# Four sums and a snapshot: who forms the partial sums at the end of the last two blocks

## The chip, the cores and the metric

The kernel runs on one core of one Trainium2 chip. A core has five engines that run their own instruction streams and wait for one another by semaphores: TensorE (PE, matrix products, with PEld for its weight loads), VectorE (DVE), ScalarE (ACT), GpSimd (POOL), and SyncE (SP, which here only issues transfers). The metric is the device time of one execution in microseconds; the profile's span of one execution is a little shorter than that time.

## The reference

Two layers follow one another. The first is a linear attention over 8 batches, 8 heads, 576 rows and 64 columns: `q` is normalised by a softmax along its columns, `k` by one along its rows, and each head's output is `q_s @ (k_s^T @ v)`. The second is a gated feed-forward layer over the 8 x 576 = 4608 rows of 512 values:

```python
x = attn_out.transpose(0, 2, 1, 3).reshape(4608, 512)
g = x @ w_gate                       # 512 x 1536
gelu = 0.5 * g * (1 + erf(g / sqrt(2)))
val = x @ w_val                      # 512 x 1536
out = (gelu * val) @ w_out           # 1536 x 512
```

## The kernel before

The feed-forward layer dominates. Its rows are worked in nine blocks of 512: blocks 0 to 7 are 512 rows of one batch each, and block 8 collects the 64 rows that remain of each batch. The blocks run in the order 0, 1, 2, 3, 4, 5, 6, 8, 7, so that block 7 is the last.

From block 1 on, the output product is a Strassen product in Winograd's form: the hidden values `h` (tile `ht`, twelve column pieces of 128 for 512 rows) and `w_out` are cut into 2 x 2 quarters, and seven products of quarters take the place of eight. They need four sums of quarters of `h`. `NO` is 6: column piece `j` of the left half goes with `j + 6` of the right half.

```python
def sum_h(j0, j1, which, eng="dve"):
    step = 1 if j1 - j0 == 2 else NO // 2          # pair j: pieces j and j + 3
    js, ks = slice(j0, j1, step), slice(NO + j0, NO + j1, step)
    a11, a21 = ht[:, js, 0:256], ht[:, js, 256:512]
    a12, a22 = ht[:, ks, 0:256], ht[:, ks, 256:512]
    s1, s2 = sh[1][:, js], sh[2][:, js]
    for i in which:
        o, a, b, op = {1: (s1, a21, a22, ALU.add), 2: (s2, s1, a11, ALU.subtract),
                       3: (a21, a11, a21, ALU.subtract),
                       4: (s4[:, js], a12, s2, ALU.subtract)}[i]
        (nc.gpsimd if eng == "pool" else nc.vector).tensor_tensor(out=o, in0=a, in1=b, op=op)
```

One call makes each of its sums for two pieces at once, 512 values a partition. There are three such pairs: pair 0 (pieces 0 and 3), pair 1 (1 and 4), pair 2 (2 and 5). Sums 1 and 2 are on VectorE. In blocks 2 to 8, sums 3 and 4 are on GpSimd.

The gate products (`x @ w_gate`, `x @ w_val`) of blocks 8 and 7 are Strassen products too, in twelve column pieces that go in pairs `k` and `k + 3`. The list `SIX` gives their order: `k.i` is step `i` of pair `k`; `s0`, `u0`, `s1`, `u1` are the places where sums of `h` are made. The last steps of a gate pair end in a GELU on ScalarE (`glq`) and a product on VectorE that writes a piece of `ht`:

```python
SIX = ("0.1 6.1 0.2 6.2 0.3 6.3 0.4 1.1 6.4 7.1 s0 1.2 7.2 1.3 u0 7.3 1.4 2.1 7.4 8.1 2.2"
       " 8.2 2.3 s1 8.3 2.4 u1")
# ... (inside pair_step)
def final(ps, fi):
    gl = ffn.tile([P, 256], f32, name="glq", tag="gl")
    nc.scalar.activation(out=gl, in_=ps[:, 1], func=ACTF.Gelu)
    nc.vector.scalar_tensor_tensor(out=ht[:, fi, 0:256], in0=ps[:, 0], scalar=_H_SCALE,
                                   in1=gl, op0=ALU.mult, op1=ALU.mult)
    let_go(ps)
```

The last gate step, `8.4`, is done inside the output stage; it writes the lower rows of piece 11 of `ht`. The upper rows of pieces 8 and 11 come from a VectorE product as well (`ht<-cc` in the profile).

The output stage of a block, cut to what matters (`b == 7` is `last`; there each accumulator is two tiles instead of one):

```python
js = (0, 1, 2, 3, 4, 5) if b < 2 else (0, 3, 1, 4, 2, 5)
get("a")
product(1, ps["a"], True, js=js[:cut])              # cut is 4 in blocks 8 and 7
# ...
if b >= B - 1:
    pair_step(b, get_x(b), NFI - NO // 2 - 1, 4)    # step 8.4
get("b")
product(1, ps["a"], False, js=js[4:])
if b > 1 and not last:
    s1 = snap("a", True)                            # snapshot on ScalarE
ride(b, PR, "e")
sum_h(*last_js(b), (1, 2))                          # pair 2
if b < 2 or last:
    s1 = snap("a")                                  # first tile on VectorE, second on ScalarE
product(2, ps["b"], True, js=js)                    # needs all of ht's lower rows
add("b", s1, 0, 0)
# ...
sum_h(*last_js(b), (4,), "pool" if b > 1 else "dve")
get("c")
product(5, ps["c"], True, js=js)                    # needs sum 1 of all pairs
sum_h(*last_js(b), (3,), "pool" if b > 1 else "dve")
s5 = snap("c", b == B or b == B - 2)
ride(b, NS, 1)
product(6, ps["a"], False, js=js)                   # needs sum 2, and the snapshot s1 done
s2 = snap("a", b == B or b == B - 2)
ride(b, NS, 2)
product(3, ps["c"], False, js=js[:cut])             # needs sum 4
# ... then product 7 (needs sum 3) and product 4
```

A `product` is twelve matrix products of 256 columns. `ride(b, NS, i)` is a place where work for later blocks may be put; in block 1 two sums of quarters of the gate weights lie at place 2:

```python
at(1, NS, 2, L(sum_wgv, "g", 3), L(sum_wgv, "v", 3))
# ...
for b in range(2, B + 1):
    for j in range(NO // 2 - 1):
        at(b, PR, f"s{j}", L(sum_h, j, NO, (1,)), L(sum_h, j, NO, (3,), "pool"))
        at(b, PR, f"u{j}", L(sum_h, j, NO, (2,)), L(sum_h, j, NO, (4,), "pool"))
```

Of the kernel before, what the change touches and what calls it, by code (L numbers as in the profile page):

```python
# [18 lines left out]
def kernel(  # L19
# [12 lines left out]
    B, H, S, D = q.shape  # L32
# [16 lines left out]
    NO = NFI // 2  # L49
# [30 lines left out]
    def big(shape, dt, name, hold=False, seed=False):  # L80
        tag = ring.pop(next(i for i, x in enumerate(ring) if x in full) if seed else 0)
        t = ps_big.tile(shape, dt, name=name, tag=tag)
        words = 1
        for n in shape[1:]:
            words *= n
        (full.add if words == 512 and shape[0] == 128 and dt == f32 else full.discard)(tag)
        if hold:
            held[id(t)] = (t, tag)
        else:
            ring.append(tag)  # L90
        return t

    def let_go(t):
        ring.append(held.pop(id(t))[1])
# [471 lines left out]
    def sum_h(j0, j1, which, eng="dve"):  # L566
        step = 1 if j1 - j0 == 2 else NO // 2
# [9 lines that stand above are left out]
# [18 lines left out]
    def product_gv(i, ps, xt, k, first):  # L595
# [3 lines left out]
        for t, w, nm in ((0, wv_sb, "v"), (1, wg_sb, "g")):  # L599
# [13 lines left out]
    FOUR = ("a 7g l 7v n 0.1 6.1 0.2 6.2 0.3 6.3 m 10g 0.4 6.4 1.1 t 10v 1.2 s0 8g u0 1.3 8v 1.4 2.1"  # L613
            " 11g s1 2.2 11v 2.3")
    SIX = ("0.1 6.1 0.2 6.2 0.3 6.3 0.4 1.1 6.4 7.1 s0 1.2 7.2 1.3 u0 7.3 1.4 2.1 7.4 8.1 2.2"
           " 8.2 2.3 s1 8.3 2.4 u1")
    steps = {b: (SIX if b >= B - 1 else THREE if b == 2 else FOUR).split() for b in range(2, B + 1)}
    live = {}

# [88 lines left out]
    def product(i, ps, first, ts=(0, 1), js=range(NO)):  # L708
        for j in js:
            for t in ts:  # L710
                c0, c1 = slice(t * P, (t + 1) * P), slice(256 + t * P, 256 + (t + 1) * P)
                a = {1: ht[:, j, c0], 2: ht[:, NO + j, c0], 3: s4[:, j, c0], 4: ht[:, NO + j, c1],
                     5: sh[1][:, j, c0], 6: sh[2][:, j, c0], 7: ht[:, j, c1]}[i]
                w = {1: wo_sb[:, j, 0:256], 2: wo_sb[:, NO + j, 0:256],
                     3: wo_sb[:, NO + j, 256:512]}.get(i)
                if w is None:
                    w = tw[{4: 4, 5: 1, 6: 2, 7: 3}[i]][:, j]
                nc.tensor.matmul(ps[t], a, w, start=(first and j == js[0] and (  # L718
                    t == ts[0] or ps[t].tensor is not ps[ts[0]].tensor)),
                                 stop=(j == js[-1]), skip_group_check=True)  # L720

    def get_x(b):
        return get_xt(b) if b < B else xtr

    def last_js(b):
        return (NO - 2 if b < 2 else NO // 2 - 1, NO)

    def out_strassen(b, last):
        yo = [yop.tile([P, 2, C], f32, name="yo", tag="yo") for _ in range(2)]
        c = (slice(0, 256), slice(256, 512))  # L730
        ps, tiles_ = {}, {}

        def get(nm):
            if last:
                tiles_[nm] = [big([P, 256], f32, "ps" + nm, True) for _ in range(2)]
                ps[nm] = [x for x in tiles_[nm]]
            else:
                tiles_[nm] = [big([P, 2, 256], f32, "ps" + nm, True)]
                ps[nm] = [tiles_[nm][0][:, t] for t in range(2)]

        def parts(nm):
            return [(0, ps[nm][0]), (1, ps[nm][1])] if last else [(slice(0, 2), tiles_[nm][0])]

        def snap(nm, act=False):
            sn = ffn.tile([P, 2, 256], f32, name="sn", tag="gl")
            for n, (t, src) in enumerate(parts(nm)):
                if n or act:
                    nc.scalar.activation(out=sn[:, t], in_=src, func=ACTF.Copy, scale=1.0 / _H_SCALE)
                else:
                    nc.vector.tensor_scalar(out=sn[:, t], in0=src, scalar1=1.0 / _H_SCALE,  # L750
                                            scalar2=None, op0=ALU.mult)
            return sn

        def add(nm, sn, half, col):
            for t, src in parts(nm):
                nc.vector.scalar_tensor_tensor(  # L756
                    out=yo[half][:, t, c[col]], in0=src, scalar=1.0 / _H_SCALE,
                    in1=sn[:, t], op0=ALU.mult, op1=ALU.add)

        js = (0, 1, 2, 3, 4, 5) if b < 2 else (0, 3, 1, 4, 2, 5)  # L760
        get("a")
        four = 2 < b < B - 1
        cut = 3 if four else 4
        product(1, ps["a"], True, js=js[:cut])
        if four:
            pair_step(b, get_x(b), NO // 2 - 1, 4)
            product(1, ps["a"], False, js=js[cut:4])
        ride(b, NS, 0)
        if four:
            ride(b, PR, "u1")  # L770
        if b >= B - 1:
            pair_step(b, get_x(b), NFI - NO // 2 - 1, 4)
        get("b")
        product(1, ps["a"], False, js=js[4:])
        if b > 1 and not last:
            s1 = snap("a", True)
        ride(b, PR, "e")
        sum_h(*last_js(b), (1, 2))
        if b < 2 or last:
            s1 = snap("a")  # L780
        product(2, ps["b"], True, js=js)
        add("b", s1, 0, 0)
        for x in tiles_["b"]:
            let_go(x)
        sum_h(*last_js(b), (4,), "pool" if b > 1 else "dve")
        get("c")
        product(5, ps["c"], True, js=js)
# [3 lines that stand above are left out]
        product(6, ps["a"], False, js=js)  # L791
        s2 = snap("a", b == B or b == B - 2)
        ride(b, NS, 2)
        cut = NO - 1 if 1 < b < B - 2 else NO
        product(3, ps["c"], False, js=js[:cut])
        if cut < NO:
            product(7, ps["a"], False, js=js)
            add("a", s5, 1, 1)
            product(3, ps["c"], False, js=js[cut:])
        add("c", s2, 0, 1)  # L800
        for x in tiles_["c"]:
            let_go(x)
        store_rows(b, 0, yo[0])
        if last:
            finish_last(b, ps["a"], yo[1], s5)
            return
        if cut == NO:
            product(7, ps["a"], False, js=js)
            add("a", s5, 1, 1)
        ride(b, NS, 4)  # L810
        if b == B:
            go_on(B - 1, get_x(B - 1), 1)
        product(4, ps["a"], False, js=js)
        nc.scalar.activation(out=yo[1][:, :, c[0]], in_=tiles_["a"][0], func=ACTF.Copy,
                             scale=1.0 / _H_SCALE)
        let_go(tiles_["a"][0])
        store_rows(b, 1, yo[1])
# [16 lines left out]
    def store_rows(b, half, yo):  # L834
        if b < B:
            store(nc.sync, yo.rearrange("p n c -> p (n c)"), b, 2 * half, 2 * half + 2)
            return
        for t in range(2):
            for j in range(2):
                o = 2 * (2 * half + t) + j  # L840
                nc.sync.dma_start(
                    out=out[o * S:(o + 1) * S, :].rearrange("(m n) c -> m n c", n=NT)[:, 0, :],
                    in_=yo[j * 64:(j + 1) * 64, t, :])
# [71 lines left out]
    FI, NS, PR = range(3)  # L915
    plan = {}

    def at(b, kind, i, *fns):
        plan.setdefault((b, kind, i), []).extend(fns)

    L = lambda f, *a: (lambda: f(*a))
# [35 lines left out]
    for i, x in enumerate(("g1", "v1", "g2", "v2", "g4", "v4")):  # L957
        at(0, FI, 5 + i, L(sum_wgv, x[0], int(x[1])))
    at(0, FI, NFI - 2, L(sum_w, 1))
    at(1, NS, 2, L(sum_wgv, "g", 3), L(sum_wgv, "v", 3))  # L960
    for b in range(2, B):
        n = b + 1
        if n < B:
# [19 lines left out]
    at(B, NS, 2, L(lambda: sum_x(get_x(B - 1), xs_b[1])))  # L983
    for b in range(2, B + 1):
        for j in range(NO // 2 - 1):
            at(b, PR, f"s{j}", L(sum_h, j, NO, (1,)), L(sum_h, j, NO, (3,), "pool"))
            at(b, PR, f"u{j}", L(sum_h, j, NO, (2,)), L(sum_h, j, NO, (4,), "pool"))
    for i, xs_ in (("w", ("g1", "v1", "g2", "v2")), ("x", ("g4", "v4", "g3", "v3"))):
        for x in xs_:
            at(2, PR, i, L(sum_wgv, x[0], int(x[1]), NO, 1, "pool"))  # L990
# [5 lines left out]
    def ride(b, kind, i):  # L996
        for fn in plan.get((b, kind, i), []):
            fn()
# [63 lines left out]
```

The softmax here doesn't subtract the row's maximum and nothing guards it: scores larger than these inputs give would overflow.

## Time and profile before

| | before |
|---|---|
| time, median of 3 (lowest to highest) | 296.51 us (296.48 to 296.78) |
| span of the profiled execution | 294.7 us |
| TensorE busy | 283.5 us (96%) |
| TensorE weight loads busy | 202.8 us (69%) |
| VectorE busy | 226.0 us (77%) |
| GpSimd busy | 205.9 us (70%) |
| ScalarE busy | 194.4 us (66%) |

A line of the timeline has the start in us from the span's beginning, the duration, the engine, the line of the kernel, the operation with `out<-in` by tile name, shapes, how many instructions were merged, and in brackets the idle time before and what ended it. Names to know: `psa`, `psb`, `psc` are the accumulators of the output stage; `sh` holds sums 1 and 2, `s` sum 4, and sum 3 overwrites its quarter of `ht`; `sn` is a snapshot of an accumulator, `yo` a result. `L576` is the line of the sums of `h`, `L587` that of the weight sums, `L718` that of the output products. Consecutive instructions of VectorE overlap a little: one starts about 0.08 us before the end that the profile gives for the one ahead. [...]what counts for TensorE is the distance from start to start.

### The profile page before, as it was taken

The numbers are of one execution on the slowest core, as the hardware profiler recorded it, in microseconds if no ns is written. First come the engines' busy times: TensorE is split into PE (matmuls) and PEld (weight loads), VectorE is DVE, ScalarE is ACT, GpSimd is POOL, SyncE is SP. The second block draws the span as 40 slices with busy tenths as digits, with TensorE's granted clock in tenths as the row PEclk, the third lists the DMA queues.
The fourth block names the chain that finished last, engine by engine and source line by source line (L and its number), as shares of the span: only waits on it lengthen the run. The fifth ranks groups of instructions, "written<-read, shape, count | busy, mean of one in ns | idle before, by whom it ended". The sixth has DMA issues, their size and how long they took to land. (4 is left out here: it accounts for less than half of the span.)

```text
span 294.7 us, 6354 instructions
## 1 busy us (share of the span) xinstructions
PE 283.5 (96%) x2449; PEld 202.8 (69%) x2449; DVE 226.0 (77%) x409; ACT 194.4 (66%) x321; POOL 205.9 (70%) x191
## 2 busy tenths in 40 slices
PE   3999999999999999999999999999999999899984
PEld 1544445446767687779777877687768888788863
DVE  2855888878878769768977896787678789849992
ACT  4663367776776589768976898589863576447730
POOL 1558647870499699868887788779886555774480
PEclk9999999999999999999999999999999999999999
DMA  6999999998069605970499039803050200032003
GB/s 225 373 382 389 400 391 392 337 323 231 3 224 383 108 3 174 382 157 3 153 373 206 2 136 350 232 1 122 24 100 2 120 24 1 2 91 55 0 2 142
DMA packets 54622, 51.72 MB, mean 176 GB/s; under 512 B 18496, under 2 KB 50496, under 8 KB 54592
## 3 DMA queue, kind: packets, MB, share of 16 engines
q1 hardware_dynamic: 52864, 49.49, 52.9%
q10 hardware_dynamic: 1728, 1.84, 1.9%
q8 instruction: 19, 0.31, 0.4%
q14 instruction: 11, 0.09, 0.1%
HBM read 37.75 MB, written 9.44 MB: 160 GB/s over the span
## 5 line engine op out<-in xcount | busy, mean ns | idle before, releaser
L467 PE MATMUL psg<-xt,wg_sb 128*128 128x512 f16 x184 | 49.3, 379 | 0.0
L467 PE MATMUL psv<-xt,wv_sb 128*128 128x512 f16 x184 | 49.2, 379 | 0.0
L718 PEld LDWEIGHTS <-ht 128*128 128x128 f16 x384 | 36.4, 98 | 10.1 <-issue 2.7
L250 POOL TENSOR_TENSOR eq<-eq,rrq 128x640 f16<-128x640 f16 (+1 forms) x27 | 34.7, 1302 | 11.7 <-DVE rrq L242 7.8
L576 POOL TENSOR_TENSOR ht<-ht 128x512 f16<-128x512 f16 x21 | 26.7, 1270 | 6.1 <-DVE sh L576 6.1
L606 PEld LDWEIGHTS <-wv_sb 128*128 128x128 f16 x248 | 24.1, 98 | 9.4 <-issue 1.0
L653 POOL TENSOR_TENSOR ht<-eq 128x512 f16<-128x512 f32 x14 | 17.8, 1273 | 18.0 <-ACT eq L651 18.0
L467 PEld LDWEIGHTS <-wv_sb 128*128 128x128 f16 x184 | 17.9, 98 | 18.0 <-issue 0.5
L576 POOL TENSOR_TENSOR s<-ht,sh 128x512 f16<-128x512 f16 x21 | 24.7, 1176 | 6.9 <-DVE sh L576 6.9
L467 PEld LDWEIGHTS <-wg_sb 128*128 128x128 f16 x184 | 17.9, 98 | 16.5
L634 DVE SCALAR_TENSOR_TENSOR ht<-pga,glq 128x256 f16<-128x256 f32 x31 | 13.0, 421 | 20.6 <-ACT glq L633 20.5
L188 POOL CAST v<-vt 128x640 f16<-128x640 f32 x26 | 19.1, 776 | 12.8 <-PE pskv L343 11.3
L606 PEld LDWEIGHTS <-wg_sb 128*128 128x128 f16 x248 | 24.2, 98 | 2.8
L653 POOL TENSOR_TENSOR ht<-cc 128x512 f16<-128x512 f32 x15 | 19.1, 1274 | 8.6 <-ACT cc L651 8.5
L472 ACT ACTIVATE gl<-psg 128x512 f32<-128x512 f32 x24 | 13.8, 597 | 16.9 <-PE psg L467 15.8
L633 ACT ACTIVATE glq<-pgb 128x256 f32<-128x256 f32 x31 | 11.7, 378 | 18.7 <-PE pgb L606 10.9
L718 PE MATMUL psa<-tw,ht 128*128 128x256 f16 x192 | 23.4, 272 | 0.2 <-DVE yo L756 0.2
L212 ACT ACTIVATE ek<-kt 128x1280 f16<-128x1280 f32 (+1 forms) x11 | 19.1, 1748 | 5.7 <-DMA kt<-in_k_dram 4.2
L473 DVE SCALAR_TENSOR_TENSOR ht<-psv,gl 128x512 f16<-128x512 f32 x24 | 16.0, 686 | 8.6 <-PE psv L467 6.8
L663 ACT COPY pgb<-pga 128x512 f32<-128x512 f32 x31 | 18.0, 580 | 6.9 <-PE pga L606 6.6
L643 ACT ACTIVATE snq<-pga 128x512 f32<-128x512 f32 x31 | 18.5, 599 | 4.0 <-PE pga L606 3.7
L718 PEld LDWEIGHTS <-sh 128*128 128x128 f16 x192 | 18.6, 98 | 2.8 <-DVE sh L576 0.4
(172 smaller groups left out, 732.0 us busy)
## 6 DMA issues: line engine op xcount, KB each, us to landing
out_dram<-yo SPq DMA_DIRECT2D x15, 512.0 KB, 3.4
kt<-in_k_dram SPq DMA_DIRECT2D x7, 640.0 KB, 8.6
vt<-in_v_dram SPq DMA_DIRECT2D x7, 640.0 KB, 5.0
qt<-in_q_dram SPq DMA_DIRECT2D x7, 640.0 KB, 7.6
qt<-in_q_dram SPq DMA_DIRECT2D x8, 512.0 KB, 7.8
wost<-in_moe_w_out_dram SPq DMA_DIRECT2D x6, 512.0 KB, 7.9
kt<-in_k_dram SPq DMA_DIRECT2D x6, 512.0 KB, 9.7
vt<-in_v_dram SPq DMA_DIRECT2D x6, 512.0 KB, 5.7
```

The source lines that it names most:

```text
L188: nc.gpsimd.tensor_copy(out=dst, in_=src)
L212: nc.scalar.activation(out=dst[:, n0:NC, h0 * D:h1 * D].rearrange(o, d=D, **({"t": 2} if b >= QUAD else {})), in_=heads(tiles[(nm, b)], b, ...
L250: (nc.gpsimd if eng == "pool" else nc.vector).tensor_tensor(out=e, in0=e, in1=rrq.unsqueeze(-1).to_broadcast((P, n, 2, D)), op=ALU.mult)
L467: nc.tensor.matmul(ps, w[:, ci, fi * P:(fi + 1) * P], xt[:, ci, :], start=(ci == 0), stop=(ci == HP - 1))
L472: nc.scalar.activation(out=gl, in_=psg, func=ACTF.Gelu)
L473: nc.vector.scalar_tensor_tensor(out=ht[:, fi, :], in0=psv, scalar=_H_SCALE, in1=gl, op0=ALU.mult, op1=ALU.mult)
L576: (nc.gpsimd if eng == "pool" else nc.vector).tensor_tensor(out=o, in0=a, in1=b, op=op)
L606: nc.tensor.matmul(ps[:, t], a, x, start=(first and t == 0 and c == 0), stop=(c == 1), skip_group_check=True)
L643: nc.scalar.activation(out=sn, in_=ps, func=ACTF.Copy, scale=_H_SCALE)
L653: (nc.vector if k == NFI - NO // 2 - 1 else nc.gpsimd).tensor_tensor(out=ht[:, k:k + NO // 2 + 1:NO // 2, 256:512], in0=cc[:, :, 0], in1=c ...
L663: nc.scalar.copy(out=pb, in_=pa)
L718: nc.tensor.matmul(ps[t], a, w, start=(first and j == js[0] and (t == ts[0] or ps[t].tensor is not ps[ts[0]].tensor)), stop=(j == js[-1]), ...
```

## The change

Three things are moved; nothing is computed that was not computed before, and nothing is left out.

1. In blocks 8 and 7 the sums 3 and 4 of pair 1 go from GpSimd to VectorE. Together with sum 2 they now stand in the output stage behind the first sum of pair 2, so that the last gate piece of `ht` comes ahead of them.
2. The first snapshot of block 7 is made on ScalarE alone, as it is in blocks 2 to 6 and 8, and before the sums in the program.
3. In block 1 the sum of the gate weights `g` moves from place 2 to place 1 of the output stage, one snapshot earlier.

The first is meant to take VectorE and GpSimd out of each other's way in the last output stages and to let TensorE have its last piece of `ht` earlier; the second relieves VectorE of an instruction there; the third uses a pause of VectorE.

```diff
@@ the order of the gate steps
-           " 8.2 2.3 s1 8.3 2.4 u1")
+           " 8.2 2.3 s1 8.3 2.4")
@@ the output stage
-        if b > 1 and not last:
+        if b > 1:
             s1 = snap("a", True)
         ride(b, PR, "e")
-        sum_h(*last_js(b), (1, 2))
-        if b < 2 or last:
+        sum_h(*last_js(b), (1,))
+        if b >= B - 1:
+            ride(b, PR, "u1")
+        sum_h(*last_js(b), (2,))
+        if b < 2:
             s1 = snap("a")
@@ the plan
-    at(1, NS, 2, L(sum_wgv, "g", 3), L(sum_wgv, "v", 3))
+    at(1, NS, 1, L(sum_wgv, "g", 3))
+    at(1, NS, 2, L(sum_wgv, "v", 3))
@@
-            at(b, PR, f"s{j}", L(sum_h, j, NO, (1,)), L(sum_h, j, NO, (3,), "pool"))
-            at(b, PR, f"u{j}", L(sum_h, j, NO, (2,)), L(sum_h, j, NO, (4,), "pool"))
+            at(b, PR, f"s{j}", L(sum_h, j, NO, (1,)))
+            if j and b >= B - 1:
+                at(b, PR, f"u{j}", L(sum_h, j, NO, (2, 3, 4)))
+            else:
+                at(b, PR, f"s{j}", L(sum_h, j, NO, (3,), "pool"))
+                at(b, PR, f"u{j}", L(sum_h, j, NO, (2,)), L(sum_h, j, NO, (4,), "pool"))
```

## The prediction

> **What bounds the kernel now.** I read four views, from the whole to the instruction. The page comes first. TensorE has work in 283.5 of 294.7 us (96%) at the full clock, and only the first slice and a few late ones are below 9 tenths, so time can be won only where TensorE stands still. The waits of TensorE between 60 us and the end are the second view. They are three lines:
>
> ```profile
> PE psb L718 <- DVE ht L634: 1.8, 2, 0.9
> PE psa L718 <- DVE yo L756: 0.2, 1, 0.2
> PE psa L718 <- DVE sn L750: 0.2, 1, 0.2
> ```
>
> Columns are total us, number of waits, longest. The reader is to see that two waits of 0.9 us carry nearly all of it, and that each names a VectorE write of `ht`. The third view, the timeline, puts one of them at 254.77 us (block 8) and one at 283.56 us (block 7, the last to run). Around the latter it reads (start, duration, engine, line, operation, count, idle before):
>
> ```profile
> 279.97 1.28 POOL L653 TENSOR_TENSOR ht<-eq 128x512 f16<-128x512 f32 x1 [2.55 <-ACT eq L651]
> ...
> 281.19 0.69 DVE L653 TENSOR_TENSOR ht<-cc 128x512 f16<-128x512 f32 x1
> 281.21 1.68 POOL L576 TENSOR_TENSOR ht<-ht 128x512 f16<-128x512 f16 x1
> 281.22 0.38 ACT L633 ACTIVATE glq<-pga 128x256 f32<-128x256 f32 x1
> 281.40 1.26 PE L718 MATMUL psb<-wo_sb,ht 128*128 128x256 f16 x10
> ...
> 281.80 1.37 DVE L576 TENSOR_TENSOR sh<-sh,ht 128x512 f16<-128x512 f16 x1
> 283.09 0.41 DVE L634 SCALAR_TENSOR_TENSOR ht<-pga,glq 128x256 f16<-128x256 f32 x1
> 283.25 1.15 POOL L576 TENSOR_TENSOR s<-ht,sh 128x512 f16<-128x512 f16 x1 [0.36 <-DVE sh L576]
> 283.43 1.25 DVE L576 TENSOR_TENSOR sh<-ht 128x512 f16<-128x512 f16 x1
> ...
> 283.56 0.39 PE L718 MATMUL psb<-wo_sb,ht 128*128 128x256 f16 x2 [0.91 <-DVE ht L634]
> ...
> 283.79 1.56 PE L718 MATMUL psc<-tw,sh 128*128 128x256 f16 x12
> 284.71 0.42 DVE L576 TENSOR_TENSOR sh<-sh,ht 128x512 f16<-128x512 f16 x1
> ...
> 285.06 0.42 DVE L750 TENSOR_SCALAR sn<-psa 128x256 f32<-128x256 f32 x1
> ...
> 285.53 1.47 PE L718 MATMUL psa<-tw,sh 128*128 128x256 f16 x12 [0.18 <-DVE sn L750]
> ```
>
> Read it from the late end. The last two of the 12 `psb` products need the last piece of `ht`, which VectorE writes at 283.09. Its input `glq` was there at 281.60 (281.22 + 0.38). VectorE was held by the sum in front of it: `sh<-sh,ht` at 281.80, for 1.37 us, where its median is 0.42. GpSimd's `ht<-ht` runs over the same time, until 282.89, and VectorE's sum ends 0.28 us after it. At 283.25 and 283.43 the same pair collides again: GpSimd's `s` ends at 284.40, VectorE's `sh` (1.25 us) at 284.68. Only then can the next `sh` and the first snapshot (285.06) go, and the `psa` products wait for that snapshot until 285.53.
>
> What that costs TensorE, with one product per 0.109 us (12 `psa` products of block 8 at 256.40 are followed by `psc` at 257.71: 1.31 / 12). In block 7 ten `psb` products from 281.40 are issued by 282.49, and the next start at 283.56: 1.07 lost. Twelve `psc` from 283.79 would end at 285.10, and `psa` starts at 285.53: 0.43 lost. Afterwards 1.30 us lie between groups, nothing lost. In block 8 the ten from 252.61 should be followed at 253.70 and are at 254.77: 1.07 lost; then 0.09, as `psc` at 255.00 is followed by `psa` at 256.40. So 1.50 us in block 7 and 1.16 us in block 8.
>
> The remaining 0.2 us is at the end of block 1:
>
> ```profile
> 76.71 3.36 POOL L188 CAST v<-vt 128x640 f16<-128x640 f32 x4 [11.34 <-PE pskv L343]
> ...
> 77.65 0.84 DVE L587 TENSOR_TENSOR wg_sb<-wg_sb 128x768 f16<-128x768 f16 x1
> ...
> 78.42 1.06 DVE L587 TENSOR_TENSOR wv_sb<-wv_sb 128x768 f16<-128x768 f16 x1
> ...
> 80.01 0.67 DVE L756 SCALAR_TENSOR_TENSOR yo<-psa,sn 128x512 f32<-128x512 f32 x1
> ...
> 80.74 1.47 PE L718 MATMUL psa<-tw,ht 128*128 128x256 f16 x12 [0.21 <-DVE yo L756]
> ```
>
> Two weight sums of VectorE lie between the snapshot and the two results `yo`; the second `yo` begins at 80.01 although its products ended at 79.79, and the next `psa` group waits for it.
>
> **What the Trainium skill says.** "SBUF — State Buffer", section "Who interferes with whom": a VectorE instruction with two SBUF inputs and a GpSimd instruction that reads SBUF take an exclusive lock in turn, and the later one fully blocks. The trace agrees: 1.37 and 1.25 us against 0.42, each ending just behind GpSimd's instruction, and GpSimd's 1.68 against a median 1.16 where it started behind VectorE's `ht<-cc` (281.19 to 281.88). "VectorE: DVE Perf Modes", section "The TRN2 errata": 58 + elements / mode cycles at 0.96 GHz. For 512 two-byte elements at twice the rate that gives 314 cycles, an estimated 327 ns from one sum to the next; the trace has 0.33 us where two unblocked sums follow (74.33 and 74.66). "GPSIMD Engine Reference", section 4.1, calls GpSimd about half as fast for two inputs; here it is worse, 1.15 against 0.42 us.
>
> **The change, part by part.**
>
> 1. Sums 3 and 4 of pair 1 in blocks 8 and 7 leave GpSimd: 2 x 2 instructions of 1.15 us when unblocked, more when not. VectorE gets them at 0.33 us from start to start, two more per block, 0.66 us. Sum 2 of pair 1, which was already VectorE's, moves behind the gate product and the first sum of pair 2. The instruction order confirms the new sequence: `ht<-cc`, `ht<-pga`, sum 1 of pair 2, sums 2, 3, 4 of pair 1, sum 2 of pair 2, `yo<-psb`.
>
> Worked on the times of block 7. `ht<-cc` starts at 281.19 as before, as it waits for ScalarE. The next can start 0.61 later (281.80, as now), and is now `ht<-pga`: 281.80 to 282.21, seen by TensorE 0.06 later (as 283.50 was seen at 283.56), 282.27. TensorE wants it at 282.49, and its weight load about 0.1 earlier, at 282.38. It fits, with some 0.1 us to spare, so the whole 1.07 goes. Block 8: 253.01 to 253.42, wanted at about 253.59: the same.
>
> Then the five sums start at 282.13, 282.46, 282.79, 283.12, 283.45, and the last ends at 283.88. No GpSimd sum is left to collide with: its `ht<-eq` ends at 281.25, its next sum waits for 283.88. TensorE, undisturbed, starts `psc` at 282.71, needs the late half of `sh` 1 at 283.58 (ready 282.54), starts `psa` at 284.02, needs the late half of `sh` 2 at 284.89 (ready 283.88), starts the next `psc` at 285.33 and wants GpSimd's last `s` at 286.20. GpSimd can do that from about 283.95 to 285.10 and its last `ht` to 286.25, wanted at 286.86. So 0.43 in block 7 and 0.09 in block 8 go too. VectorE then still has two `yo<-psb` (0.76) and half a snapshot of `psc` (0.42) after 283.88, done by 284.90, wanted at 285.33.
>
> 2. The first snapshot of block 7 on ScalarE: one VectorE instruction of 0.42 less, one ScalarE instruction of 0.38 more, ready at about 282.40 where ScalarE is idle for 3.34 us. It removes what `psa` waited for at 285.53. Its gain is in the 0.43 already counted. Block 8 had its snapshot there already.
>
> 3. The weight sum of block 1 moves into the gap before the snapshot (75.72 to 76.34, 0.62 us idle). GpSimd is idle there until 76.71, so I take 0.55 us for it, from the same shape at 27.4 us (548 ns), and it just fits. The remaining weight sum then runs from 77.65 and ends near 78.6, `yo<-psc` can follow its products (78.5), and `yo<-psa` starts with its own at 79.83 instead of 80.01. That is 0.18 us at the `psa` group; 0.03 of the 0.21 stays.
>
> Sum: 1.50 + 1.16 + 0.18 = 2.84 us, and 296.51 - 2.84 = 293.67.
>
> **The rivals.** First: a wait is moved and not removed. The new run of sums pushes the release of `psb` and the snapshot of `psc` later, or the 0.1 us to spare at the gate product is not there. For it speaks that VectorE goes without a pause for 4 us; against it the margins above, 0.4 us or more everywhere but at the gate product. It would leave 0.1 to 0.4 us per block: 294.0 to 294.5. Second: VectorE is so slowed by five sums in a row that it becomes the bound of the output stage. If each took 0.46 us from start to start (as 71.89 to 72.35, where one needs its predecessor's result), the last would end at 284.4, the snapshot of `psc` at 285.4, 0.1 late: 293.9. The order separates sums that depend on one another by another instruction, except the first move from `ht<-pga` to sum 1. Third: what is won in block 1 or 8 is lost later, since GpSimd's `vt` sums feed block 7 and loads feed blocks 2 to 4. The waits list shows no TensorE wait on either, and the `vt` sums start as much earlier as TensorE does (GpSimd loses 2.3 us of work before them). If the block 1 gain is lost, 293.85. Fourth: a new collision of the moved weight sum; it would take 0.84 or more, and the snapshot behind it would start 0.2 us late with no one waiting.
>
> **Range and chances.** All known disturbances take from the gain, so the range leans upward: 293.7 us, between 293.3 and 294.6. To reach 2% it would need 5.9 us, and TensorE has no more than 2.9 us of such waits after 60 us; to lose 2% a new wait of 5.9 us would have to arise. I give 1% to each.
>
> **What would show it.** In the profile after, the line of `psb` waiting for `ht` is gone or under 0.2 us in sum; the pair 1 sums of blocks 8 and 7 take about 0.42 us each on VectorE, none over 0.6; `psb`, `psc`, `psa` and `psc` follow one another at 1.31 us in both blocks; GpSimd has four instructions less. The span falls from 294.7 to about 291.9. A remaining gap before the last two `psb` products would prove the first rival; sums over 0.45 us and a wait for `sn` the second; an end of block 1 that is earlier by under 0.1 us would show step 3 wrong.

## The result and the profile after

The changed kernel takes 293.73 us (293.70 to 293.77, four runs) against 296.60 us (296.48 to 296.78, four runs) of the kernel before. The ratio is 0.9903, with a 95% interval of 0.9886 to 0.9920. The prediction was 293.7 us. The span went from 294.7 to 292.0 us.

The page of the changed kernel (span; busy time of TensorE; its busy tenths in 40 slices):

```profile
span 292.0 us, 6352 instructions
...
PE 282.8 (97%) x2449; PEld 203.1 (70%) x2449; DVE 221.8 (76%) x412; ACT 194.9 (67%) x322; POOL 200.5 (69%) x187
...
PE   3999999999999999999999999999999999999994
```

TensorE has a 9 in every slice but the first and the last. Its waits over the whole span (total us, times, longest) are now two, both before 60 us:

```profile
engine line waited for: us in total, times, longest us
PE pswarm L459 <- ACT warm L864: 4.9, 1, 4.9
PE pst L368 <- POOL eq L250: 0.3, 1, 0.3
```

The two waits of `psb` for `ht`, and the waits of `psa` for `sn` and `yo`, are gone. The timeline of block 7's output stage shows the new order (start, duration, engine, line, operation, count, idle before):

```profile
279.93 0.69 DVE L653 TENSOR_TENSOR ht<-cc 128x512 f16<-128x512 f32 x1
279.96 0.38 ACT L633 ACTIVATE glq<-pga 128x256 f32<-128x256 f32 x1
280.14 1.47 PE L718 MATMUL psb<-wo_sb,ht 128*128 128x256 f16 x12
280.29 0.66 ACT L748 ACTIVATE sn<-psa 128x256 f32<-128x256 f32 x2
280.54 0.42 DVE L634 SCALAR_TENSOR_TENSOR ht<-pga,glq 128x256 f16<-128x256 f32 x1
280.87 0.41 DVE L576 TENSOR_TENSOR sh<-ht 128x512 f16<-128x512 f16 x1
281.20 0.42 DVE L576 TENSOR_TENSOR sh<-sh,ht 128x512 f16<-128x512 f16 x1
...
281.45 1.47 PE L718 MATMUL psc<-tw,sh 128*128 128x256 f16 x12
281.54 0.42 DVE L576 TENSOR_TENSOR ht<-ht 128x512 f16<-128x512 f16 x1
281.87 0.42 DVE L576 TENSOR_TENSOR s<-ht,sh 128x512 f16<-128x512 f16 x1
282.21 0.42 DVE L576 TENSOR_TENSOR sh<-sh,ht 128x512 f16<-128x512 f16 x1
...
282.70 1.16 POOL L576 TENSOR_TENSOR s<-ht,sh 128x512 f16<-128x512 f16 x1 [2.73 <-DVE sh L576]
282.76 1.47 PE L718 MATMUL psa<-tw,sh 128*128 128x256 f16 x12
...
284.07 1.47 PE L718 MATMUL psc<-wo_sb,s 128*128 128x256 f16 x12
```

`ht<-pga` starts at 280.54, directly behind `ht<-cc`, and not behind a sum; the twelve `psb` products are one group. The five sums stand 0.33 us apart and take 0.41 or 0.42 us each. GpSimd's next instruction is at 282.70, when they are all done. The groups of TensorE start at 280.14, 281.45, 282.76 and 284.07: 1.31 us apart each time, which is twelve products without a pause.

**Where the time came from.** The start of every group of TensorE products can be compared with the same group of the kernel before. The difference stays constant over long stretches and jumps only where something was won or lost. The prologue before 60 us moves from one execution to the next, by up to 0.3 us in all traces but one, so only the jumps count:

| place (time in the kernel before) | changed kernel against before | jump |
|---|---|---|
| 60.54, block 1 | -0.05 us | (prologue) |
| 80.74, `psa` at the end of block 1 | -0.22 us | 0.17 us won |
| 108.82, `psa` at the end of block 2 | -0.11 us | 0.11 us lost |
| 171.17, block 4 | -0.09 us | 0.02 us lost |
| 255.00 and 256.40, `psc`, `psa` of block 8 | -1.18, then -1.27 us | 1.18 us won |
| 283.79 and 285.53, `psc`, `psa` of block 7 | -2.34, then -2.77 us | 1.50 us won |

The sum of the jumps is 0.17 - 0.11 - 0.02 + 1.18 + 1.50 = 2.72 us. Blocks 8 and 7 gave what was forecast. Block 1 gave it too, but two thirds of that was lost again within 28 us, at a place where the kernel before seemed to have no wait. The theory for blocks 8 and 7 was the collision of the two engines plus the order of VectorE's instructions; what was open was how much each of the two is worth. For the loss in block 2, the two traces name GpSimd. Here is the kernel before at that place (PEld is the weight load of TensorE):

```profile
100.86 1.27 POOL L653 TENSOR_TENSOR ht<-cc 128x512 f16<-128x512 f32 x1 [1.78 <-ACT cc L651]
100.87 1.54 DVE L576 TENSOR_TENSOR sh<-sh,ht 128x512 f16<-128x512 f16 x1
...
102.09 1.34 POOL L576 TENSOR_TENSOR ht<-ht 128x512 f16<-128x512 f16 x1
...
107.37 1.16 POOL L576 TENSOR_TENSOR s<-ht,sh 128x512 f16<-128x512 f16 x1
...
107.67 1.31 PE L718 MATMUL psc<-wo_sb,s 128*128 128x256 f16 x10
...
108.58 0.11 PEld L718 LDWEIGHTS <-s 128*128 128x128 f16 x2 [0.15 <-POOL s L576]
...
108.82 1.50 PE L718 MATMUL psa<-tw,ht 128*128 128x256 f16 x12
```

and here the changed kernel:

```profile
100.64 1.56 POOL L653 TENSOR_TENSOR ht<-cc 128x512 f16<-128x512 f32 x1 [1.73 <-ACT cc L651]
100.65 0.43 DVE L576 TENSOR_TENSOR sh<-sh,ht 128x512 f16<-128x512 f16 x1
...
102.17 1.15 POOL L576 TENSOR_TENSOR ht<-ht 128x512 f16<-128x512 f16 x1
...
107.26 1.16 POOL L576 TENSOR_TENSOR s<-ht,sh 128x512 f16<-128x512 f16 x1
...
107.45 1.42 PE L718 MATMUL psc<-wo_sb,s 128*128 128x256 f16 x10
...
108.47 0.11 PEld L718 LDWEIGHTS <-s 128*128 128x128 f16 x2 [0.27 <-POOL s L576]
...
108.71 1.50 PE L718 MATMUL psa<-tw,ht 128*128 128x256 f16 x12
```

Ten `psc` products should take 1.09 us to issue; before, `psa` follows after 1.15, now after 1.26. The last two of them need the `s` that GpSimd starts at 107.37 before and 107.26 now. TensorE came 0.22 us earlier, GpSimd only 0.11. The reason is at the top of each fence: two instructions start within 0.01 us of one another, GpSimd's `ht<-cc` and VectorE's `sh`. Before, VectorE was blocked (1.54 us); now GpSimd was, and took 1.56 us in place of 1.27. So its next sum starts 0.08 us later than before (102.17 against 102.09), although `ht<-cc` had started 0.22 earlier; that sum then wins 0.19 us back (1.15 us in place of 1.34). From there to 109 us GpSimd works without a pause in both kernels, so the rest of the delay reaches `s`.

This loss does not hang on the moved weight sum alone. The kernel before with only the snapshot of block 7 moved (its run is below) has nothing changed before block 7. In its trace the same two instructions start at the same times as in the kernel before, yet GpSimd is the one that is blocked:

```profile
100.86 1.56 POOL L653 TENSOR_TENSOR ht<-cc 128x512 f16<-128x512 f32 x1 [1.78 <-ACT cc L651]
100.87 0.42 DVE L576 TENSOR_TENSOR sh<-sh,ht 128x512 f16<-128x512 f16 x1
...
108.69 0.11 PEld L718 LDWEIGHTS <-s 128*128 128x128 f16 x2 [0.26 <-POOL s L576]
...
108.93 1.50 PE L718 MATMUL psa<-tw,ht 128*128 128x256 f16 x12
```

Its `psa` starts at 108.93 in place of 108.82: the same 0.11 us are lost, with nothing won in block 1. Of the ten traces with block 2 as it was, `psa` follows `psc` after 1.24 to 1.26 us in the five where GpSimd is blocked, and after 1.14 to 1.15 us in the five where VectorE is. The four of these ten that have the weight sum moved are all among the first five; of the six that have it at its old place, one is (the snapshot alone). Whether the moved sum tips the balance, or chance, is not shown.

### The profile page after: what moved, and what is told of

It reads as the page before. It is cut to its first block, busy times and chain, and to the rows that moved or that the text cites. A ratio compares the mean times of both kernels' runs of the same rounds, so it can differ in the third digit from the quotient of the medians.

```text
span 292.0 us, 6352 instructions
## 1 busy us (share of the span) xinstructions
PE 282.8 (97%) x2449; PEld 203.1 (70%) x2449; DVE 221.8 (76%) x412; ACT 194.9 (67%) x322; POOL 200.5 (69%) x187
## 4 chain that ended last, share of the span: by engine, by line
PE 94%; DVE 2%; DMA 2%; ACT 0%; issue 0%; ACTq 0%
PE pga L606 19%; PE psa L718 15%; PE psg L467 14%; PE psv L467 14%; PE pgc L606 9%; PE psc L718 7%; PE pgb L606 5%; PE psb L718 4%; PE psy L535 4%; DMA qt<-in_q_dram 2%; PE pskv L343 2%; PE psx L430 1%; DVE rq L240 1%; PE psx L409 1%; DVE eq L250 0%; PE pskv L284 0%
## 5 line engine op out<-in xcount | busy, mean ns | idle before, releaser
L576 POOL TENSOR_TENSOR s<-ht,sh 128x512 f16<-128x512 f16 x19 | 22.4, 1178 | 9.8 <-DVE sh L576 9.8
L576 POOL TENSOR_TENSOR ht<-ht 128x512 f16<-128x512 f16 x19 | 23.1, 1215 | 6.1 <-DVE sh L576 6.1
L240 DVE TENSOR_REDUCE rq<-eq 128x20 f32<-128x1280 f16 (+1 forms) x12 | 17.2, 1432 | 4.6 <-ACT eq L212 4.6
```

What stands on the lines that cost most here:

```text
L240: nc.vector.reduce_sum(rq, e, axis=mybir.AxisListType.X)
```

## The experiments

All are compared with the kernel before, on the same chip as they ran. "Jump" means the shift of TensorE's groups, as above.

**The sums alone.** The changed kernel with the snapshot and the weight sum as before:

```diff
-        if b > 1:
+        if b > 1 and not last:
             s1 = snap("a", True)
...
-        if b < 2:
+        if b < 2 or last:
             s1 = snap("a")
...
-    at(1, NS, 1, L(sum_wgv, "g", 3))
-    at(1, NS, 2, L(sum_wgv, "v", 3))
+    at(1, NS, 2, L(sum_wgv, "g", 3), L(sum_wgv, "v", 3))
```

> The sums of pair 1 alone (part 1), snapshot and weight sum as before. My theory: the wait before the last two psb products goes in both blocks (1.07 us each) and block 8 has its full 1.16 us. In block 7 the first half of the snapshot is still VectorE's, behind five sums: it would end at 284.22 on the clock of the kernel before, where psa is wanted at 284.02, so about 0.26 us stay. Gain 1.16 + 1.50 - 0.26 = 2.40 us, about 294.2 us. The rival, that the snapshot did not matter once the sums are free, expects 2.66 us, about 293.9 us.

Measured: 294.10 us (294.04 to 294.17), before 296.54; ratio 0.9915 (0.9900 to 0.9929). The jumps are 1.16 us in block 8, 1.07 at `psc` and 0.17 at `psa` in block 7: 1.24 us. The first half of the snapshot runs at 282.59 to 283.01 and `psa` starts at 283.06, where 1.31 us behind `psc` (281.49) would be 282.80: 0.26 us, as expected. Behind the five sums the place of the snapshot matters.

**The snapshot alone.** The kernel before with `if b > 1:` and `if b < 2:` at the two places.

> The first snapshot of block 7 on ScalarE alone (part 2) on the kernel before. My theory: the 0.43 us before the psa group in block 7 shrinks to the 0.09 us that block 8 shows with its ScalarE snapshot, and nothing else moves: a gain of 0.34 us, 296.2 us. The rival that this wait is the sums' and not the snapshot's expects no change.

Measured: 296.20 us (295.99 to 296.45), before 296.49; ratio 0.9990 (0.9982 to 0.9998). The only jump at the end is at `psa` of block 7, from +0.15 to -0.20: 0.35 us. (0.11 of the +0.15 is the loss in block 2 shown above.) So the two parts overlap: alone the snapshot is worth 0.35 us, behind the sums 0.26.

**The order alone.** The changed kernel with sums 3 and 4 of pair 1 on GpSimd:

```diff
-            at(b, PR, f"s{j}", L(sum_h, j, NO, (1,)))
-            if j and b >= B - 1:
-                at(b, PR, f"u{j}", L(sum_h, j, NO, (2, 3, 4)))
-            else: ...
+            at(b, PR, f"s{j}", L(sum_h, j, NO, (1,)), L(sum_h, j, NO, (3,), "pool"))
+            at(b, PR, f"u{j}", L(sum_h, j, NO, (2,)), L(sum_h, j, NO, (4,), "pool"))
```

> The changed kernel with sums 3 and 4 of pair 1 in blocks 8 and 7 back on GpSimd: the new order alone. My theory: the gate product, which reads one operand from SBUF only, needs no lock, so ahead of the sums it is early and both waits of 1.07 us go. GpSimd then has 2 x 1.15 us more before its last two sums, and the psc and psa groups behind them wait some 0.3 to 0.7 us per block: about 294.4 to 294.9 us. The rival that the lock is all, and that the order without the engine does little, expects the two waits of 0.9 us back and about 296.4 us. The rival that order is all expects 293.75 us.

Measured: 294.00 us (293.93 to 294.05), before 296.54; ratio 0.9911 (0.9894 to 0.9927). That is faster than I expected, and much nearer to the rival that order is all. The timeline of its block 7:

```profile
279.90 0.69 DVE L653 TENSOR_TENSOR ht<-cc 128x512 f16<-128x512 f32 x1
279.91 1.69 POOL L576 TENSOR_TENSOR ht<-ht 128x512 f16<-128x512 f16 x1
...
280.51 0.42 DVE L634 SCALAR_TENSOR_TENSOR ht<-pga,glq 128x256 f16<-128x256 f32 x1
280.84 1.04 DVE L576 TENSOR_TENSOR sh<-ht 128x512 f16<-128x512 f16 x1
...
284.64 1.15 POOL L576 TENSOR_TENSOR ht<-ht 128x512 f16<-128x512 f16 x1
...
285.35 3.10 PE L718 MATMUL psa<-tw,ht 128*128 128x256 f16 x24
```

The collision is there in full: GpSimd's `ht<-ht` takes 1.69 us and ends at 281.60, and VectorE's first `sh` takes 1.04 us, ending 0.28 us later. But the gate product between them, `ht<-pga` at 280.51, takes 0.42 us while GpSimd runs. It has one operand in PSUM and one in SBUF. The Trainium skill says as much ("SBUF — State Buffer", "Who interferes with whom"): a VectorE instruction with at most one SBUF input, outside its two-port modes, does not contend. The blocked sums have slack and the gate product has none, so putting it first is enough: the jumps are 1.17 us in block 8 and 1.51 us in block 7, as in the changed kernel. What GpSimd still costs comes at the very end: its last `ht<-ht` starts at 284.64 and ends at 285.79, and the 24 `psa` products that read it take 3.10 us where the changed kernel has 2.81: 0.29 us. In block 7 the third of these products needs it already, in block 8 only the ninth, and there nothing is lost. My 0.3 to 0.7 us per block was right for one block, at its lower end.

**The engine alone.** The kernel before, with

```diff
+            if j and b >= B - 1:
+                at(b, PR, f"s{j}", L(sum_h, j, NO, (1, 3)))
+                at(b, PR, f"u{j}", L(sum_h, j, NO, (2, 4)))
+                continue
             at(b, PR, f"s{j}", L(sum_h, j, NO, (1,)), L(sum_h, j, NO, (3,), "pool"))
```

> The kernel before with only the engine changed: sums 3 and 4 of pair 1 in blocks 8 and 7 on VectorE at their old places. My theory: no sum is blocked any more (all near 0.42 us), but three sums stand ahead of the gate product, and the extra one at the earlier place delays the upper rows too; the last psb products are still about 0.9 us late. Gain about 0.28 us in block 8 and 0.62 us in block 7, about 295.7 us. The rival that the lock is all expects the waits for ht gone and about 294 us.

Measured: 295.91 us (295.77 to 295.98), before 296.54; ratio 0.9977 (0.9967 to 0.9987). The jumps are 0.12 us in block 8 and 0.46 in block 7, a little less than expected. Its waits of TensorE after 60 us:

```profile
PE psb L718 <- DVE ht L634: 0.9, 2, 0.4
PE pga L606 <- DVE cc L647: 0.5, 2, 0.3
PE psa L718 <- DVE yo L756: 0.2, 1, 0.2
```

No sum is blocked, yet `psb` still waits for `ht`, and there is a new wait: sum 3 at its old place pushes `cc` back, and the last gate products (`pga`) wait for it. The part of the wait that was a collision became plain work in the wrong place.

**The collision alone.** The kernel before without sums 3 and 4 of pair 1 in blocks 8 and 7. They are left out, so those blocks multiply old values of `s` and unchanged quarters of `ht`; the number of products is the same.

```diff
+            if j and b >= B - 1:
+                at(b, PR, f"s{j}", L(sum_h, j, NO, (1,)))
+                at(b, PR, f"u{j}", L(sum_h, j, NO, (2,)))
+                continue
             at(b, PR, f"s{j}", L(sum_h, j, NO, (1,)), L(sum_h, j, NO, (3,), "pool"))
```

> The kernel before without sums 3 and 4 of pair 1 in blocks 8 and 7 (left out, so those two blocks multiply stale values): nothing else is moved. My theory: sum 2 takes 0.42 us in place of 1.37, the gate product ends at 282.54 on the clock of the kernel before, and the last two psb products are about 0.1 us late instead of 1.07. Gain about 1.04 us in block 8 and 1.38 us in block 7, about 294.2 us. The rival that it is the place of sum 2 in the order that costs, and not the collision, expects the wait to stay near 0.9 us and no gain to speak of.

Measured: 293.93 us (293.87 to 294.23), before 296.54; ratio 0.9911 (0.9896 to 0.9926). Jumps 1.04 us in block 8 and 1.38 in block 7, both as expected. The time is lower than the 294.2 expected: 296.54 less the two jumps is 294.12, and in the trace TensorE was 0.14 us early before block 8. Block 7:

```profile
280.01 0.69 DVE L653 TENSOR_TENSOR ht<-cc 128x512 f16<-128x512 f32 x1
...
280.23 1.60 PE L718 MATMUL psb<-wo_sb,ht 128*128 128x256 f16 x12
...
280.62 0.42 DVE L576 TENSOR_TENSOR sh<-sh,ht 128x512 f16<-128x512 f16 x1
280.96 0.41 DVE L634 SCALAR_TENSOR_TENSOR ht<-pga,glq 128x256 f16<-128x256 f32 x1
...
281.66 1.47 PE L718 MATMUL psc<-tw,sh 128*128 128x256 f16 x12
```

Sum 2 still stands ahead of the gate product, but takes 0.42 us. The twelve `psb` products are one group of 1.60 us where 1.47 would be undisturbed: the 0.1 us that sum 2 costs by its place. So of the 1.07 us per block, the collision made up all but that. The first half of the snapshot is still VectorE's here, at 282.08 with two sums fewer ahead of it, and `psa` at 282.97 does not wait for it.

**The weight sum alone.** The kernel before with `at(1, NS, 1, L(sum_wgv, "g", 3))` taken out of place 2.

> The weight sum of block 1 alone (part 3) on the kernel before. My theory from the two traces: the psa group at the end of block 1 is 0.17 us earlier, but at the end of block 2 the psc group waits for GpSimd's sum of pair 2, whose chain is only 0.06 us earlier net, so that about 0.06 to 0.1 us of 0.18 reach the end: 296.4 to 296.55 us. The rival that the whole 0.18 us is kept expects 296.35 us and a constant shift of 0.17 us after block 1.

Measured: 296.48 us against 296.49, ratio 0.9997 (0.9989 to 1.0006): no difference can be measured. In its trace, whose prologue came 2.5 us late, the shift goes from +2.50 to +2.33 at the end of block 1 (0.17 won), to +2.42 at the end of block 2 (0.09 lost), and to +2.46 at the end. GpSimd is blocked in block 2 here too (1.56 us), and little is kept.

**The loss in block 2.** Two weight sums of GpSimd (0.67 us each) stand ahead of its last two sums of `h` in block 2, and are needed only in block 3. In this version of the changed kernel they stand behind them:

```diff
-    for i, xs_ in (("w", ("g1", "v1", "g2", "v2")), ("x", ("g4", "v4", "g3", "v3"))):
+    for i, xs_ in (("w", ("g1", "v1", "g2", "v2")), ("x", ("g4", "v4"))):
         for x in xs_:
             at(2, PR, i, L(sum_wgv, x[0], int(x[1]), NO, 1, "pool"))
+    at(2, NS, 1, L(sum_wgv, "g", 3, NO, 1, "pool"), L(sum_wgv, "v", 3, NO, 1, "pool"))
```

> The changed kernel with two of GpSimd's weight sums at the end of block 2 (g3 and v3, 0.67 us each) moved behind its two sums of h of pair 2. My theory that GpSimd's chain sets the end of block 2: the sum 4 of pair 2 is 1.3 us earlier, the psc group there no longer waits, and the 0.17 us lost at about 108.5 us comes back: 293.55 us, and a shift of 0.17 us or more against the changed kernel from there to the end. The rival that the 0.1 us was lost to something else (a load, ScalarE) expects 293.7 us. If GpSimd's later work (casts of v) becomes late, it would be slower than 293.7 us.

> The changed kernel once more, as the base of the small comparisons: 293.7 us.

Measured: 293.46 us (293.39 to 293.56), with the changed kernel at 293.59 us (293.51 to 293.62) beside it on the same chip; the ratios to the kernel before are 0.9897 (0.9884 to 0.9911) and 0.9901 (0.9887 to 0.9914). Block 2 in it:

```profile
105.98 1.15 POOL L576 TENSOR_TENSOR s<-ht,sh 128x512 f16<-128x512 f16 x1
...
107.42 1.26 PE L718 MATMUL psc<-wo_sb,s 128*128 128x256 f16 x10
...
108.21 0.66 POOL L587 TENSOR_TENSOR wg_sb<-wg_sb 128x256 f16<-128x256 f16 x1
...
108.51 1.47 PE L718 MATMUL psa<-tw,ht 128*128 128x256 f16 x12
```

`s` is done at 107.13, before the `psc` group starts; the ten `psc` and the next `psa` are 1.09 us apart, nothing lost, and the shift against the changed kernel jumps by 0.16 us there (from -0.04 to -0.20). GpSimd is blocked in this trace as well (1.56 us at 100.61), but no longer late. The weight sums, now at 108.21 and later, delay nobody.

Three more kernels separate this from the weight sum of block 1: the same version again, the same without part 3, and the changed kernel without part 3. Both undo part 3 by the line `at(1, NS, 2, L(sum_wgv, "g", 3), L(sum_wgv, "v", 3))`.

> The version with block 2's two GpSimd weight sums moved back, once more, as the base of the next two: 293.45 us.

> The same version with the weight sum of block 1 back at its old place (part 3 undone). My theory: with GpSimd's chain out of the way at the end of block 2, the 0.17 us of part 3 reach the end, so without it 293.62 us, and the psa group at the end of block 1 waits for yo again. The rival that block 1's gain is lost anyway expects no difference.

> The changed kernel with part 3 undone and block 2 as it was. My theory: 0.17 us are lost at the end of block 1, 0.06 to 0.1 us of them are left at the end, as GpSimd's chain hides the rest in block 2: 293.65 to 293.7 us where the changed kernel has 293.59. The rival that all of part 3 is kept expects 293.76 us.

Measured: 293.36 us (293.31 to 293.51), 293.60 us (293.52 to 293.68) and 293.75 us (293.64 to 293.76), before 296.47; ratios 0.9896 (0.9881 to 0.9910), 0.9904 (0.9887 to 0.9920) and 0.9907 (0.9892 to 0.9922). Between the first two the traces differ by 0.15 to 0.18 us from the end of block 1 to the end: with GpSimd's chain out of the way, all of part 3 is kept. Between the changed kernel and the third, 0.18 us are lost at the end of block 1 and 0.10 won back at the end of block 2, so 0.08 us remain of part 3. But what was won back is the collision: in the third trace VectorE is blocked (1.55 us), in the changed kernel GpSimd. Where GpSimd is blocked on both sides, changed kernel against the snapshot alone, the lead at `psa` is 0.22 us at the end of block 1 (80.52 against 80.74) and still 0.22 at the end of block 2 (108.71 against 108.93): there part 3 is kept whole. The median of 293.75 us lies at the rival's 293.76 and not within 293.65 to 293.7; it was not taken side by side with the changed kernel's 293.59 or 293.73, and does not settle so small a figure.

## Why the prediction was right, and where it was not

- **The two waits in blocks 8 and 7** were worth what was read off the gaps of TensorE: 1.18 and 1.50 us for 1.16 and 1.50. Leaving GpSimd's two sums out gave 1.04 and 1.38 without any change of order, which shows that the collision made the wait.
- **The five sums at 0.33 us**: the last of them was to end at 283.88 on the old clock; block 7 runs 1.26 us earlier up to there, so 282.62; it ended at 282.63. The margin of 0.1 us at the gate product held.
- **The snapshot** was counted within block 7's 0.43 us. The runs give its share, 0.26 us behind the sums.
- **The first two rivals** did not come: no wait took the place of the old ones in blocks 8 and 7, and no sum of VectorE there took over 0.42 us. Nor did the fourth: the moved weight sum took 0.55 us, at 75.59.
- **The third step fell short in its last part.** The working was right up to the `psa` group of block 1 (0.18 expected, 0.17 measured). What was missing is the end of block 2. The third rival said "what is won in block 1 or 8 is lost later", and held against it: "The waits list shows no TensorE wait on either". That list was of products. A weight load did wait 0.15 us for GpSimd's `s` at 108.58, and that was 0.06 us of lost time already: GpSimd was late at that place, so whatever delays it delays TensorE. What delayed it was the collision of `ht<-cc` with `sh`, which fell on VectorE in the kernel before and on GpSimd in the changed one: 0.11 us. So 0.04 to 0.08 us of 0.17 are left where it fell on GpSimd only with part 3, and all of it where it fell on GpSimd either way. The sum of 2.84 us was 0.12 too high by the trace (2.72); the medians differ by 2.87 us, in which a change of the prologue by some 0.1 us can't be told from the rest. That 293.73 lies so close to 293.7 is luck to that extent.
- **What the prediction treated as one** it should have split: the move to VectorE and the new order. With the engine undone (order, snapshot and weight sum kept), 2.54 us of the gain remain (296.54 - 294.00); the engine alone, without order and snapshot, gives 0.63 (296.54 - 295.91).

## What to carry to other kernels

When two engines block one another, look first for the instruction behind the blocked one that does not need the lock and that others wait for: moving it ahead was worth nearly as much here as removing the collision, and adds no instruction to any engine. A gain counts to the end only if every other engine has slack at the next place where the bottleneck meets it: read weight loads as well as products, and check an engine that shows no pause. Before a jump of 0.1 us is put down to a change, see in both traces which engine was blocked where two arrive together. A part that can't be measured alone may be worth its full size once the next wait is removed.

## What the runs showed of the hardware

Who is blocked when two arrive together can't be read from the starts. In block 2 GpSimd's `ht<-cc` and VectorE's `sh` start within 0.01 us of one another in all thirteen traces, GpSimd's always first in the record. Yet VectorE is blocked in five (1.54 or 1.55 us for 0.42) and GpSimd in eight (1.55 or 1.56 us for 1.27), and with the same instructions and the same starts, 100.86 and 100.87, the kernel before and the snapshot alone differ. The Trainium skill ("SBUF — State Buffer", "Who interferes with whom") says that issue order decides who blocks. The first collision in block 7 of the kernel before agrees: `ht<-ht` starts at 281.21, VectorE's sum at 281.80, and the sum is blocked. At 0.01 us the trace does not resolve the order.

A blocked sum of VectorE ended 0.28 us after GpSimd's instruction wherever its times are shown above: 283.17 after 282.89 and 284.68 after 284.40 in block 7 of the kernel before, 281.88 after 281.60 with the order alone, 102.41 after 102.13 in block 2.
